# Float32 weights in two VectorE operations on 512-column tiles, and the first block's queries loaded four tokens to a row

## The chip, the cores and the metric

The kernel runs on one core of a Trainium2 chip. The metric is device time in microseconds, the median of several executions of one program; less is better. The profile comes from one execution.

## The reference

Attention over pooled keys and values, then two feed-forward layers, all in float32 on 4608 tokens of 512 features:

```python
# q, k, v: batch 8, heads 8, seq 576, head_dim 64; keys and values are pooled by 8, so 72 of each
k_p = k.reshape(B, H, Sp, 8, D).mean(axis=3)
v_p = v.reshape(B, H, Sp, 8, D).mean(axis=3)
scores = scale * np.matmul(q, k_p.transpose(0, 1, 3, 2))
attn = softmax(scores)                      # less the maximum, 1e-9 added to the sum
x = (attn @ v_p) -> (4608, 512)
h = x @ w_in                                # 512 x 2048
x = (h * np.clip(h + 3.0, 0.0, 6.0) / 6.0) @ w_out
g = x @ w_gate                              # 512 x 1536
out = (g * sigmoid(g) * (x @ w_val)) @ w_out2
```

The weights arrive as float64: each is two 32-bit words, and the kernel makes float32 of them on the chip.

## The kernel before

The tokens are cut into nine blocks of 512. **Startup** computes attention for block 0, in units of two heads (a pair, four pairs in all) and 256 tokens. In **block j** the first feed-forward layer runs over 16 slices f of 128 hidden columns: `up` (12 matmuls of 512 columns, line 553) makes a slice, `act1` and `split_g` its activation and its high and low part, and `down1` (12 matmuls) adds the slice of two steps earlier to four PSUM accumulators. Between them `attn_slot` puts the attention steps of block j + 1. Block 8 has no attention beside it. After block 8 (1040.6 us) the second layer runs on seven products in place of eight (lines 660 to 783).

A float32 matmul is made of three `float32r` matmuls on high and low parts (`mm3`), so every weight is split: ScalarE casts it to the high part, another engine subtracts (line 137).

Weights of the first layer come in during startup and block 0, by the class `Weights`. Its `todo` lists pieces of 256 columns (`WC`), two to each slice of `w_in` and two to each of `w_out`. They go through four stages: `fetch` starts a DMA into a tile of the pool `stg` (six tiles); `rescale` (line 115) has ScalarE multiply the upper words, read as float32, by 2^-112 in place; `join` (lines 117 to 133) has VectorE put the upper and lower words together with three integer operations; `split` casts on ScalarE and subtracts on GpSimd. Each call of `convert(2)` moves two pieces by one stage: it splits those joined in the call before, joins those rescaled, rescales two staged ones and refills the staging tiles. The joined pieces lie in the tiles `w32` of pool `t` (two buffers). Startup calls `convert` six times as step C of its plan, then until the second slice of `w_in` is there; block 0 calls it twice in each f. The high and low parts of `w_out` are also stored to DRAM (`w1d`) and read again in each later block.

Weights of the second layer are prepared in blocks 1 to 8 by `prep_slot`: 18 units, six f apart, of four quarters with 256 columns each; a unit is fetched, rescaled, joined (step 2), summed on GpSimd, cast on ScalarE and subtracted on VectorE, and stored.

All engines take their instructions in the order in which the program writes them. The order of attention steps comes from two tables (`when_startup`, `when`, lines 823 to 832): a unit i puts a step at slot i plus a lag, sorted by the second number within the slot. In startup a slot holds among others: X (exponentials of the unit before), T (transposes of the attention weights), K and P (transposes of a pair's pooled keys and of its queries), C (convert), V (attend), S (scores and their maximum).

The queries of the first block's four pairs are fetched by `load_first` (line 337): four DMAs a pair, each 512 tokens by 32 features, so rows of 128 bytes; the first two pairs' first two go out from ScalarE's queue, the others from SyncE's (SP). VectorE turns them with one transpose of 32 x 32 blocks (line 432) into `qT`, features by tokens. In startup the PSUM pool `ps_a` (two banks, tag `att`) serves only the transposes of the keys.

## Time and profile before

| | us |
|---|---|
| median of 3 runs | 1835.23 (1834.75 to 1835.96) |
| profiled execution | 1835.06 |
| its span, first to last instruction | 1833.3 |
| TensorE busy | 1748.5 (95%) |
| VectorE busy | 1258.8 (69%) |
| ScalarE busy | 686.8 (37%) |
| GpSimd busy | 676.6 (37%) |

The names in rows are those of the program: PE is TensorE, PEld its weight loads, DVE VectorE, ACT ScalarE, POOL GpSimd, SP SyncE; `L131` is line 131; `w<-wstg,w` writes tile `w` (for `w32`) and reads `wstg` and `w`. Idle time of an engine that is not the bottleneck costs nothing. An execution takes 1.8 us more than the span.

### The profile page before, as it was taken

How to read it: one execution, taken by the hardware profiler on the slowest of the kernel's cores; microseconds unless marked ns; L12 is line 12 of the kernel's file. 1: busy time of each engine (PE TensorE's matmuls, PEld its weight loads, DVE VectorE, ACT ScalarE, POOL GpSimd, SP SyncE). 2: the span in 40 equal slices, each digit the busy share in tenths (PEclk: the TensorE clock that was granted, in tenths of full speed). 3: DMA queues.
4: the chain of work that ended last, by engine and by line, in shares of the span. 5: the costliest groups of instructions: out<-in, count | busy, mean ns of one | idle time of the engine just before them, and what ended most of it. 6: DMA issues, size and time to landing. Idle time of an engine off the chain costs nothing.

```text
span 1833.3 us, 28479 instructions
## 1 busy us (share of the span) xinstructions
PE 1748.5 (95%) x9929; PEld 1575.9 (86%) x9929; DVE 1258.8 (69%) x2480; ACT 686.8 (37%) x1612; POOL 676.6 (37%) x833
## 2 busy tenths in 40 slices
PE   4687899999999998999999999999999999999999
PEld 3476688888878787878888899999999999999999
DVE  6787676876767677686542367767678668568666
ACT  5444344443444444444433223224224225124223
POOL 5455342331423325233114154153252352361450
PEclk8888999999999999999999999999999999999999
DMA  7555456665766656656553487887887977977876
GB/s 159 173 174 162 148 172 200 216 185 183 215 206 197 197 168 195 209 159 197 194 177 132 177 294 238 296 288 241 305 277 252 315 262 250 324 252 253 284 245 219
DMA packets 203103, 402.97 MB, mean 220 GB/s; under 512 B 90576, under 2 KB 126416, under 8 KB 192208
## 3 DMA queue, kind: packets, MB, share of 16 engines
q1 hardware_dynamic: 198256, 396.17, 66.9%
q10 hardware_dynamic: 4704, 4.98, 0.9%
q8 instruction: 79, 1.29, 0.3%
q14 instruction: 64, 0.52, 0.1%
HBM read 340.79 MB, written 60.29 MB: 219 GB/s over the span
## 4 chain that ended last, share of the span: by engine, by line
PE 81%; DVE 7%; DMA 5%; issue 2%; POOL 2%; ACT 2%; SPq 1%; ACTq 0%; POOLq 0%; DVEq 0%
PE b L660 43%; PE y L553 17%; PE h L553 16%; PE pss L445 2%; DMA y<-yo 1%; DVE w L126 1%; DVE w L131 1%; DMA vts<-in_v_dram 1%; PE pst L505 1%; DMA qs<-in_q_dram 1%; DVE w L120 1%; PE pst L509 1%; DVE kp L370 1%; DMA fly<-w1d 1%; PE psk L393 1%
## 5 line engine op out<-in xcount | busy, mean ns | idle before, releaser
L660 PE MATMUL b<-xc,wr 128*128 128x384 f32 x3024 | 525.2, 334 | 0.0
L660 PEld LDWEIGHTS b<-xc,wr 128*128 128x128 f32 x3024 | 524.0, 188 | 0.1
L553 PE MATMUL h<-x,wu 128*128 128x512 f32 x1728 | 435.3, 401 | 0.0
L553 PE MATMUL y<-g,fly 128*128 128x512 f32 x1728 | 430.2, 398 | 1.5 <-DMA fly<-w1d 0.8
L669 DVE TENSOR_TENSOR c<-c,b 128x384 f32<-128x384 f32 x504 | 265.2, 552 | 178.5 <-PE b L660 154.7
L553 PEld LDWEIGHTS h<-x,wu 128*128 128x128 f32 x1728 | 322.0, 191 | 65.3 <-DVE x L546 0.6
L553 PEld LDWEIGHTS y<-g,fly 128*128 128x128 f32 x1728 | 318.3, 189 | 66.4 <-ACT yo L594 1.0
L707 POOL TENSOR_TENSOR s<-s,c 128x384 f32<-128x384 f32 x144 | 142.4, 1013 | 400.2 <-ACT s L705 400.2
L660 PE MATMUL b<-wr,gc 128*128 128x256 f32 x2268 | 265.6, 279 | 0.0
L660 PEld LDWEIGHTS b<-wr,gc 128*128 128x128 f32 x2268 | 265.4, 188 | 0.0
L488 POOL TENSOR_TENSOR e<-e,sm 96x288 f32<-96x288 f32 (+3 forms) x85 | 73.5, 865 | 451.9 <-DVE sm L484 336.1
L714 POOL TENSOR_TENSOR gf<-s,c 128x384 f32<-128x384 f32 x144 | 168.2, 1192 | 67.3 <-DVE c L669 66.5
L136 ACT CAST gc<-gf 128x768 fp32r<-128x768 f32 x126 | 105.7, 839 | 186.6 <-POOL gf L714 101.0
L705 ACT ACTIVATE s<-c 128x384 f32<-128x384 f32 x144 | 73.5, 526 | 202.0 <-DVE c L669 200.9
L137 DVE TENSOR_TENSOR gc<-gf,gc 128x768 fp32r<-128x768 f32 x126 | 133.9, 1095 | 15.5 <-ACT gc L136 13.7
L137 DVE TENSOR_TENSOR g<-g,g 128x512 fp32r<-128x512 f32 x128 | 93.0, 727 | 67.1 <-ACT g L136 66.6
L577 DVE SCALAR_TENSOR_TENSOR g<-t,h 128x512 f32<-128x512 f32 x144 | 97.3, 676 | 59.9 <-ACT t L575 53.5
L136 ACT CAST g<-g 128x512 fp32r<-128x512 f32 x144 | 88.6, 615 | 85.5 <-PE y L553 46.0
L575 ACT ACTIVATE t<-h,three 128x512 f32<-128x512 f32 x144 | 98.2, 682 | 37.1 <-PE h L553 36.4
L475 ACT ACTIVATE e<-e 96x288 f32<-96x288 f32 (+3 forms) x85 | 35.3, 415 | 185.2 <-DVE e L472 183.9
L445 PE MATMUL pss<-kbd,qT 128*128 128x144 f32 (+2 forms) x336 | 63.2, 308 | 29.3 <-DVE x L546 26.4
L677 ACT COPY c<-b 128x384 f32<-128x384 f32 x72 | 33.9, 471 | 145.6 <-PE b L660 145.6
(106 smaller groups left out, 1723.0 us busy)
## 6 DMA issues: line engine op xcount, KB each, us to landing
wr<-sup SPq DMA_DIRECT2D x72, 1024.0 KB
fly<-w1d SPq DMA_DIRECT2D x128, 512.0 KB
wr<-sdn SPq DMA_DIRECT2D x84, 768.0 KB
wr<-sup SPq DMA_DIRECT2D x72, 768.0 KB
sup<-s SPq DMA_DIRECT2D x12, 1792.0 KB
wstg<-in_moe_w_out_dram SPq DMA_DIRECT2D x56, 256.0 KB
sdn<-s SPq DMA_DIRECT2D x6, 1792.0 KB
ystg<-y SPq DMA_DIRECT2D x24, 384.0 KB
```

Of the source, the lines that this page charges most:

```text
L136: nc.scalar.copy(out=hi, in_=src)
L137: lo_engine.tensor_tensor(out=lo, in0=src, in1=f32(hi), op=ALU.subtract)
L445: nc.tensor.matmul(out=ps[:, i], lhsT=qT[:, i * qt:(i + 1) * qt], rhs=kbd_t[p], start=True, stop=True)
L488: nc.gpsimd.tensor_tensor(out=e3, in0=e3, in1=sm.to_broadcast(list(e3.shape)), op=ALU.mult)
L553: nc.tensor.matmul(out=ps, lhsT=w(kt, wh), rhs=x(kt, xh), start=first and n == 0, stop=last and n == 3 * len(kts) - 1,)
L575: nc.scalar.activation(out=t, in_=ps, func=ACTF.Relu, bias=three)
L577: nc.vector.scalar_tensor_tensor(out=g, in0=t, scalar=6.0, in1=ps, op0=ALU.min, op1=ALU.mult)
L660: nc.tensor.matmul(out=ps, lhsT=w(wh), rhs=x(xh), start=first and n == 0, stop=last and n == 2)
L669: add = lambda dst, a, b: nc.vector.tensor_tensor(out=dst, in0=a, in1=b, op=ALU.add)
L705: nc.scalar.activation(out=g[q], in_=c[q], func=ACTF.Sigmoid)
L707: nc.gpsimd.tensor_tensor(out=g[q], in0=g[q], in1=c[q], op=ALU.mult)
L714: nc.gpsimd.tensor_tensor(out=gf[p][:, GP[TURN[q]], f], in0=g[q], in1=c[q], op=ALU.mult)
```

## The change

- A piece is 512 columns, a whole slice: `WC` is 512, `stg` has three tiles, `convert(1)` moves one piece by one stage. Each of `w_in`'s and `w_out`'s 32 slices is one DMA.
- `rescale` uses the function `Prelu` in place of `Copy`: positive values are multiplied by 2^-112, negative ones by 2^-112 times 2^32. `join` then needs one shift by 3 to the left and one operation that shifts the lower word and combines it; the third operation, which put the sign back, is gone.
- The units of the second layer take two staging tiles of two quarters each, by the same four DMAs, and join two quarters at once into two places of `q7`.
- The queries of the first block's four pairs come in one DMA a pair, four tokens (1 KB) of one head to a partition. `prep_q` turns them for these pairs with eight TensorE matmuls against the identity into one PSUM bank, and VectorE copies the bank to `qT` with the tokens back in order.

```diff
@@ -77,7 +77,7 @@
...
     prep_ctx = ExitStack()
-    stg_p = prep_ctx.enter_context(tc.tile_pool(name="stg", bufs=6, side="right"))
+    stg_p = prep_ctx.enter_context(tc.tile_pool(name="stg", bufs=3, side="right"))
     q7_p = prep_ctx.enter_context(tc.tile_pool(name="q7", bufs=1, side="right"))
@@ -97,40 +97,38 @@
     wu = {}
-    WC = 256
+    WC = 512
     def fetch(src):
         t = stg_p.tile([P, WC, 2], F32, tag="stg", name="wstg")
+        fetch_into(t, src)
+        return t
+    def fetch_into(t, src):
         nc.sync.dma_start(
...
         )
-        return t
     def rescale(stage):
         hi = stage[:, :, 1]
-        nc.scalar.activation(out=hi, in_=hi, func=ACTF.Copy, scale=2.0 ** -112)
-    def join(pieces):
-        for stage, dst in pieces:
-            hi = stage[:, :, 1].bitcast(I32)
-            nc.vector.tensor_scalar(
-                out=dst, in0=hi, scalar1=4, scalar2=1,
-                op0=ALU.logical_shift_left, op1=ALU.logical_shift_right,
-            )
-        for stage, dst in pieces:
-            lo = stage[:, :, 0].bitcast(I32)
-            nc.vector.scalar_tensor_tensor(
-                out=dst, in0=lo, scalar=29, in1=dst, op0=ALU.logical_shift_right, op1=ALU.bitwise_or
-            )
-        for stage, dst in pieces:
-            hi = stage[:, :, 1].bitcast(I32)
-            nc.vector.scalar_tensor_tensor(
-                out=dst, in0=hi, scalar=-(2 ** 31), in1=dst, op0=ALU.bitwise_and, op1=ALU.bitwise_or
-            )
+        nc.scalar.activation(out=hi, in_=hi, func=ACTF.Prelu, scale=2.0 ** -112, alpha=2.0 ** 32)
+    def join(stage, dst, parts=1):
+        hi, lo = (stage[:, :, i].bitcast(I32) for i in (1, 0))
+        if parts > 1:
+            hi, lo = (t.rearrange("p (k n) -> p k n", k=parts) for t in (hi, lo))
+        nc.vector.tensor_scalar(
+            out=dst, in0=hi, scalar1=3, scalar2=None, op0=ALU.logical_shift_left,
+        )
+        nc.vector.scalar_tensor_tensor(
+            out=dst, in0=lo, scalar=29, in1=dst, op0=ALU.logical_shift_right, op1=ALU.bitwise_or
+        )
     def split(hi, lo, src, lo_engine):
@@ -141,50 +139,36 @@
...
             self.todo, self.staged, self.scaled, self.joined = [], [], [], []
-            self.cur = {}
         def add_up(self, key, src, f):
             w = src.bitcast(I32).rearrange("(k p) f -> p k f", p=P)[:, :, 2 * P * f:2 * P * (f + 1)]
-            for i in range(KT * P // WC):
-                m = WC // P
-                self.todo.append(("up", key, w[:, m * i:m * (i + 1)], i))
+            self.todo.append(("up", key, w))
         def add_down(self, key, src, f):
-            w = src.bitcast(I32)[f * P:(f + 1) * P, :]
-            for i in range(DM // WC):
-                self.todo.append(("down", key, w[:, 2 * WC * i:2 * WC * (i + 1)], i))
+            self.todo.append(("down", key, src.bitcast(I32)[f * P:(f + 1) * P, :]))
         def fetch(self):
-            while self.todo and len(self.staged) + len(self.scaled) < 6:
+            while self.todo and len(self.staged) + len(self.scaled) < 3:
                 item = self.todo.pop(0)
...
             done, self.joined = self.joined, []
-            for (kind, key, _, i), t in done:
-                if i == 0:
-                    if kind == "up":
-                        self.cur[key] = wu_p.tile([P, 2, KT, P], F32R, tag="wu", name="wu")
-                    else:
-                        self.cur[key] = fly_p.tile([P, 2, DM], F32R, tag="fly", name="fly")
-                w = self.cur[key]
+            for (kind, key, _), t in done:
                 if kind == "up":
+                    w = wu[key] = wu_p.tile([P, 2, KT, P], F32R, tag="wu", name="wu")
                     w = w.rearrange("p a k f -> p a (k f)")
-                w = w[:, :, WC * i:WC * (i + 1)]
+                else:
+                    w = fly[key] = fly_p.tile([P, 2, DM], F32R, tag="fly", name="fly")
                 split(w[:, 0], w[:, 1], f32(t), nc.gpsimd)
-                if i == KT * P // WC - 1:
-                    t = self.cur.pop(key)
-                    (wu if kind == "up" else fly)[key] = t
-                    if kind == "down":
-                        nc.sync.dma_start(out=w1_d[key[1]], in_=f32(t))
-            pieces = []
+                if kind == "down":
+                    nc.sync.dma_start(out=w1_d[key[1]], in_=f32(w))
             scaled, self.scaled = self.scaled, []
...
                 t = t_p.tile([P, WC], I32, tag="w32", name="w32")
-                pieces.append((s, t))
+                join(s, t)
                 self.joined.append((item, t))
-            join(pieces)
             for item, s in self.staged[:n]:
@@ -222,6 +206,7 @@
...
     PREP = 6
+    WH = WC // 2
     prep_t = {}
@@ -236,21 +221,26 @@
...
             prep_t["q", u] = []
-            for quarter in ("11", "12", "21", "22"):
-                r, c = int(quarter[0]) - 1, int(quarter[1]) - 1
-                if kind == "up":
-                    w = (w_gate, w_val)[m].bitcast(I32).rearrange("(k p) f -> p k f", p=P)
-                    src = w[:, 2 * c:2 * c + 2, 2 * P * (2 * f + r):2 * P * (2 * f + r + 1)]
-                else:
-                    w = w_out2.bitcast(I32)[P * (2 * f + r):P * (2 * f + r + 1), :]
-                    src = w[:, 4 * P * c:4 * P * (c + 1)]
-                prep_t["q", u].append((fetch(src), place[quarter]))
+            for pair in ((("11", "21"), ("12", "22")) if kind == "up" else (("11", "21"), ("22", "12"))):
+                t = stg_p.tile([P, WC, 2], F32, tag="stg", name="wstg")
+                for i, quarter in enumerate(pair):
+                    r, c = int(quarter[0]) - 1, int(quarter[1]) - 1
+                    if kind == "up":
+                        w = (w_gate, w_val)[m].bitcast(I32).rearrange("(k p) f -> p k f", p=P)
+                        src = w[:, 2 * c:2 * c + 2, 2 * P * (2 * f + r):2 * P * (2 * f + r + 1)]
+                    else:
+                        w = w_out2.bitcast(I32)[P * (2 * f + r):P * (2 * f + r + 1), :]
+                        src = w[:, 4 * P * c:4 * P * (c + 1)]
+                    fetch_into(t[:, WH * i:WH * (i + 1)], src)
+                a, b = (place[quarter] for quarter in pair)
+                prep_t["q", u].append((t, slice(a, b + 1, b - a)))
         elif step == 1:
...
         elif step == 2:
-            q = prep_t["f", u] = q7_p.tile([P, 8, WC], F32, tag="q7", name="q7")
-            join([(s, q[:, i].bitcast(I32)) for s, i in prep_t.pop(("q", u))])
+            q = prep_t["f", u] = q7_p.tile([P, 8, WH], F32, tag="q7", name="q7")
+            for s, at in prep_t.pop(("q", u)):
+                join(s, q[:, at].bitcast(I32), 2)
         elif step == 3:
@@ -258,7 +248,7 @@
...
         elif step == 4:
-            q, t = prep_t["f", u], s7_p.tile([P, 7, 2, WC], F32R, tag="s7", name="s7")
+            q, t = prep_t["f", u], s7_p.tile([P, 7, 2, WH], F32R, tag="s7", name="s7")
             prep_t["s", u] = t
@@ -284,6 +274,7 @@
...
     MAXQ = 2
+    QJ = N // P
     kbd_t = [a_p.tile([P, K2], F32, name=f"kbd{p}") for p in range(KT)]
@@ -333,8 +324,11 @@
...
             k_t[0, p] = [ks[p][:SP_, h2] for h2 in range(2)]
-            t = qs[p // 2][:, p % 2].rearrange("p o (c d) -> p (o c) d", d=32)
-            fetch_q(t, (0, p, 0, seg_n), [nc.scalar, nc.scalar, nc.sync, nc.sync] if p < 2 else sync4)
+            t = qs[p // 2][:, p % 2].rearrange("p (h j) d -> p h j d", h=2)
+            (nc.scalar if p == 0 else nc.sync).dma_start(
+                out=t.rearrange("p h j d -> p h (j d)"),
+                in_=q[0, 2 * p:2 * p + 2, :seg_n].rearrange("h (p j) d -> p h (j d)", p=P),
+            )
             q_t[0, p, 0, seg_n] = t
@@ -429,6 +423,17 @@
...
         t = a_p.tile([P, N // 32, 32], F32, tag="qT", name="qT", bufs=2)
+        if seg in segs[:KT]:
+            s, ps = q_t.pop(seg), psum("k", [P, QJ, P])
+            for j in range(QJ):
+                for h2 in range(2):
+                    nc.tensor.matmul(
+                        out=ps[D * h2:D * (h2 + 1), j], lhsT=s[:, h2, j], rhs=ident, start=True, stop=True
+                    )
+            qT_t[seg] = t.rearrange("p c s -> p (c s)")
+            nc.vector.tensor_copy(out=qT_t[seg].rearrange("d (p j) -> d j p", j=QJ), in_=ps)
+            return
         nc.vector.transpose(out=t[:, :n // 32], in_=q_t.pop(seg)[:, :n // 32])
@@ -946,7 +951,7 @@
...
         elif what == "C":
-            weights.convert(2)
+            weights.convert()
         elif what == "E":
@@ -993,7 +998,7 @@
...
         while ("in", 1) not in wu:
-            weights.convert(2)
+            weights.convert()
         def attn_slot(j, s):
@@ -1033,7 +1038,7 @@
...
             g = act1(hp)
-            weights.convert(2 if j == 0 else 0)
+            weights.convert(1 if j == 0 else 0)
             if n >= 2:
@@ -1041,7 +1046,7 @@
...
             split_g((1, j, f), g)
-            weights.convert(2 if j == 0 else 0)
+            weights.convert(1 if j == 0 else 0)
             if j > 0:
```

## Rows read from the trace of the kernel before

**Rows 1.** The page, second part: TensorE's busy share in the span's 40 equal slices (45.8 us each), in tenths, 9 for 90% and more.

```profile
...
PE   4687899999999998999999999999999999999999
...
```

**Rows 2.** Busy time of each engine by stretch: the stretch and its length, then busy us and number of instructions of TensorE's matmuls, its weight loads, VectorE, ScalarE and GpSimd, then the granted TensorE clock, the DMA queues' busy share and GB/s. The stretches are startup, block 0, blocks 1, 2 and 5 and, last, blocks 1 to 6 together.

```profile
...
0.00:56.40 56.40, 26.24 (x112) 18.97 (x113) 38.05 (x117) 30.07 (x139) 29.29 (x63) 0.80 0.78 167
56.40:212.20 155.80, 120.53 (x578) 96.68 (x578) 121.21 (x287) 71.63 (x214) 86.44 (x119) 0.90 0.51 161
212.20:317.20 105.00, 104.19 (x521) 86.13 (x520) 74.65 (x173) 44.44 (x120) 34.63 (x55) 1.00 0.58 181
317.20:421.60 104.40, 103.28 (x517) 85.98 (x516) 78.09 (x186) 47.55 (x125) 34.84 (x58) 1.00 0.64 194
630.40:741.80 111.40, 104.82 (x517) 85.87 (x516) 78.83 (x186) 47.00 (x125) 40.13 (x58) 1.00 0.60 184
...
212.20:849.90 637.70, 622.27 (x3069) 512.90 (x3068) 462.00 (x1060) 272.76 (x719) 212.85 (x332) 1.00 0.63 193
...
```

**Rows 3.** Groups of VectorE's instructions in block 0: line, engine, operation, tiles, shapes and count, then busy us, mean ns of one, and idle us in front of them with what ended it.

```profile
...
L120 DVE TENSOR_SCALAR w<-wstg 128x256 int32<-128x256 int32 x56 | 31.4, 600 | 26.6 <-POOL wu L137 18.2 <-POOL fly L137 5.4 <-DMA q_in<-in_q_dram 2.8
L131 DVE SCALAR_TENSOR_TENSOR w<-wstg,w 128x256 int32<-128x256 int32 x56 | 27.6, 531 | 0.0
L126 DVE SCALAR_TENSOR_TENSOR w<-wstg,w 128x256 int32<-128x256 int32 x56 | 25.7, 497 | 0.0
...
```

**Rows 4.** Who waited for whom in block 0: us in all, times, longest us.

```profile
...
PE pss L445 <- DVE x L546: 20.6, 6, 4.7
...
DVE w L120 <- POOL wu L137: 18.2, 11, 2.8
...
DVE w L120 <- POOL fly L137: 5.4, 8, 1.0
...
```

**Rows 5.** Single lines over the whole span: engine, operation, tiles and count, then min/median/max ns of one, first and last start in us, shapes.

```profile
L120 DVE TENSOR_SCALAR w<-wstg x64: 279/797/1371, 34.3 to 203.2; 128x256 int32<-128x256 int32 x64
...
L131 DVE SCALAR_TENSOR_TENSOR w<-wstg,w x64: 408/412/1779, 35.7 to 205.5; 128x256 int32<-128x256 int32 x64
...
L577 DVE SCALAR_TENSOR_TENSOR g<-t,h x144: 651/678/691, 64.4 to 1033.2; 128x512 f32<-128x512 f32 x144
...
L137 POOL TENSOR_TENSOR wu<-w,wu x32: 716/728/926, 38.9 to 199.0; 128x256 fp32r<-128x256 f32 x32
...
L137 POOL TENSOR_TENSOR g<-g,g x16: 1252/1295/1584, 66.9 to 213.1; 128x512 fp32r<-128x512 f32 x16
```

**Rows 6.** Groups of GpSimd's instructions in block 0, columns as in rows 3.

```profile
...
L137 POOL TENSOR_TENSOR fly<-w,fly 128x256 fp32r<-128x256 f32 x30 | 21.6, 741 | 15.9 <-ACT fly L136 15.9
L137 POOL TENSOR_TENSOR wu<-w,wu 128x256 fp32r<-128x256 f32 x28 | 20.3, 747 | 4.2 <-ACT wu L136 4.2
...
```

**Rows 7.** The chain of waits in order of time, from 0 to 260 us: start us, us, what, here two pieces of TensorE.

```profile
...
92.90 3.65 PE psk L393 x32
...
239.26 2.75 PE h L553 x12
...
```

**Rows 8.** Groups of the whole span with different shapes kept apart, columns as in rows 3.

```profile
...
L115 ACT ACTIVATE wstg<-wstg 128x256 f32<-128x256 f32 x136 | 49.7, 430 | 0.0
...
L126 DVE SCALAR_TENSOR_TENSOR q<-wstg,q 128x256 int32<-128x256 int32 x72 | 28.4, 453 | 0.0
...
L131 DVE SCALAR_TENSOR_TENSOR q<-wstg,q 128x256 int32<-128x256 int32 x72 | 26.1, 421 | 0.0
...
L120 DVE TENSOR_SCALAR q<-wstg 128x256 int32<-128x256 int32 x72 | 21.4, 357 | 0.0
...
L592 DVE TENSOR_SCALAR yo<-y 128x512 f32<-128x512 f32 x18 | 12.1, 684 | 5.0 <-PE y L553 4.9
...
L968 ACT ACT_TABLE_LOAD x1 | 1.3, 1283 | 0.8 <-PEq L1107 0.8
...
L1051 ACT ACT_TABLE_LOAD x1 | 1.3, 1283 | 0.0
...
```

**Rows 9.** The chain of waits by line, as shares of a stretch: first from 0 to 34.2 us, then from 34 to 56.4 us (SPq and ACTq are the engines' own DMA queues, issue is time in which the profile shows no wait).

```profile
by line: DMA qs<-in_q_dram 32.5%; DMA wstg<-in_moe_w_out_dram 15.7%; DMA vt<-in_v_dram 12.7%; SPq L311 11.7%; DMA q_in<-in_q_dram 9.2%; SPq L104 7.3%; SPq L312 2.2%; issue 2.1%; ACT L968 1.7%; ACTq L361 1.5%; SPq L361 0.9%; DVE qT L432 0.7%
...
by line: DVE w L120 13.2%; DVE w L126 12.7%; DVE w L131 11.1%; issue 9.0%; POOL wu L137 6.5%; DVE x L546 6.0%; ACT es L468 5.9%; DVE mx L451 5.1%; ACT wu L136 4.0%; DVE aT L525 4.0%; POOL fly L137 3.1%; DVE es L472 2.9%; PE psv L532 2.6%; P
...
```

**Rows 10.** Busy time by stretch in startup, columns as in rows 2.

```profile
...
0.00:10.00 10.00, 2.39 (x9) 2.13 (x9) 4.27 (x13) 2.11 (x5) 3.92 (x14) 1.00 0.88 119
...
20.00:30.00 10.00, 6.08 (x37) 4.30 (x36) 8.36 (x23) 7.88 (x41) 7.44 (x16) 1.00 1.01 251
...
```

**Rows 11.** The DMA queues from 0 to 10 us: packets, bytes and how many packets are small.

```profile
...
DMA packets 3643, 1.19 MB, mean 119 GB/s; under 512 B 3253, under 2 KB 3253, under 8 KB 3643
...
```

**Rows 12.** Groups of the first 36 us with shapes kept apart, columns as in rows 3.

```profile
...
L445 PE MATMUL pss<-kbd,qT 128*128 128x144 f32 x32 | 7.6, 383 | 2.9 <-ACT kbd L399 2.9
...
L432 DVE STREAM_TRANSPOSE qT<-qs 128x512 f32<-128x512 f32 x4 | 2.8, 702 | 0.0
...
```

**Rows 13.** What TensorE waited for from 212 to 1040 us: us in all, times, longest us.

```profile
...
PE pss L445 <- DVE x L546: 5.7, 6, 2.1
PE psv L534 <- DVE vtl L424: 4.3, 3, 2.5
...
```

## Prediction

> **What bounds the kernel now.** Three views are enough, in this order. The page's forty slices [rows 1] show TensorE at 4 to 8 tenths in the first five slices and at 9 after that, so nearly all that can be gained lies in the first 230 us. The stretches [rows 2], cut at the first `up` matmul of each block, put numbers on it: startup lasts 56.4 us, block 0 lasts 155.8 us with 35.3 us of TensorE idle and a granted clock of 0.90, while block 1 lasts 105.0 us at clock 1.00 and is TensorE's own. The six blocks that convert second-layer weights (212.2 to 849.9 us) hold 15.4 us of TensorE idle together.
>
> The third view says what holds block 0. VectorE is busy for 121.2 us [rows 2]; the three lines of `join` are 31.4 + 25.7 + 27.6 = 84.7 us of that, and VectorE waits 26.6 us more in front of line 120, the first of them [rows 3]. 121.2 + 26.6 is 148 of 155.8 us: VectorE is the bound there. The wait is mostly for GpSimd's low-part subtraction of the piece joined before (18.2 + 5.4 us) [rows 4]: a `convert` makes two pieces and there are two `w32` buffers, so each join writes over a piece that GpSimd still reads. TensorE then waits behind the joins: 20.6 us for VectorE's line 546, which stands after them in the queue [rows 4].
>
> **The change, part by part.**
>
> *Joins of block 0.* 56 records of each line are 28 converts. One costs VectorE 84.7 / 28 = 3.02 us now, plus 26.6 / 28 = 0.95 us of waiting. After, it is one shift and one or-combination on 512 columns. The combination is the operation of line 577 at its width: 0.68 us (bounds: 0.65, that line's minimum; 0.82, twice the 0.41 of 256 columns) [rows 5]. The shift on 512 columns has no row: 0.28 us if width cost nothing, 0.56 us for two of 256; I take the middle, 0.42. That is 1.10 us undisturbed, 28 x 1.10 = 31 us. With one piece per convert and two buffers, a join only needs the subtraction of the piece before the last, a whole convert earlier, so I let the 23.6 us of waiting for GpSimd go.
>
> Undisturbed is too good: line 120 takes 0.28 us at best and 0.80 us at the median, and one GpSimd subtraction (0.73 us) lies between [rows 5]. Some of that collision is built in today, since the join starts when the first of two subtractions ends and the second begins. After, GpSimd has 86.4 - 41.9 + 28 x 1.30 = 81 us of work in block 0 (its 512-column subtraction takes 1.30 us) [rows 2, 5, 6]. At some 70% load and 1 us an operation, an operation of VectorE that arrives anywhere loses about 0.35 to 0.45 us: 56 of them, 20 to 25 us. VectorE then needs 121.2 - 84.7 + 31 + 0 to 25 = 67 to 92 us.
>
> The Trainium skill has a rule that speaks against the change (SBUF — State Buffer, "Who interferes with whom"): GpSimd and a VectorE operation in a two-port mode or with two SBUF inputs lock each other out for a whole instruction. By it GpSimd's operations of double width block for longer, and at its worst that is rival B, 1813 us. The trace agrees that such a lock exists (line 120 at 0.28 and at 0.80 us), and its medians for the combinations, at their undisturbed 0.41, say that it is rarely met there.
>
> TensorE's floor in block 0: 192 `up` and 168 `down` matmuls at 2.75 us per 12 are 82.5 us; the 96 records that pool three heads' keys, at 3.65 us per 32, are 10.9 us; the attention of block 1's kind is 104.2 - 384 / 12 x 2.75 = 16.2 us [rows 2, 7]. Sum 109.6 us. The worst later block (630.4 to 741.8 us) idles 6.6 us with VectorE at 71% [rows 2]; I give block 0 the same: 116 us, so **39.6 us less**. If TensorE still waited for line 546 as long as today (20.6 us), 130 us; if nothing stalls it, 109.6.
>
> What covers the rest of block 0: ScalarE is busy 71.6 of 155.8 us, and one `Prelu` on 512 columns for two copies of 0.43 us [rows 8] lies between 0.43 (width free) and twice 0.86; 28 x 0.86 = 24 us at worst would still fit beside TensorE. Casts and subtractions of 512 cost a little less than two of 256 and are counted above. Staging keeps its bytes (three tiles of 512 for six of 256) and its look-ahead of two converts; SP issues half the weight DMAs, but a tile is asked for and released as one.
>
> *Joins of startup.* Four converts join between 34.0 and 56.4 us. The three lines hold 13.2 + 12.7 + 11.1 = 37.0% of the chain in these 22.4 us, 8.3 us, and GpSimd's subtractions another 9.6%, 2.2 us [rows 9]. Four joins at 1.10 us, without GpSimd and some issue time around it, make it **7 us less** (bounds 0, if units hang on something else, and 10).
>
> *Queries of the first block.* 16 DMAs of 64 KB in 128-byte rows become four of 256 KB in 1 KB rows; SP issues three instead of twelve. In 0 to 10 us the queues are 88% busy and move 119 GB/s, in 20 to 30 us they are full at 251 GB/s [rows 10]. At the second rate (4.0 us per MB) the 0.77 MB of larger packets of the first stretch take 3.1 us, so its 3253 small ones [rows 11] took 5.7 us. 8192 of them are 14 us; as large packets the 1.05 MB are 4.2 us: up to 10 us of DMA time saved. The chain to 34 us is nearly all DMA and SP [rows 9]. But TensorE gets eight fp32 matmuls per pair, 64 records in all (16 matmuls of line 393 show 32 records): 7.3 us at 114 ns each [rows 7], 15 us at the 237 ns of line 445 in startup [rows 12]. Behind them in TensorE's queue stand the pair's key transpose, the attend of an earlier unit and the scores, and ScalarE's exponentials wait for those. The VectorE copy out of PSUM (512 columns, like line 592's 0.68 us) replaces a transpose of 0.70 us [rows 8, 12], so nothing is saved there. The PSUM bank comes from the two that only key transposes use in startup, and is asked for once per pair, so I give it nothing. Bounds -10 and +15. VectorE is busy 8.4 and ScalarE 7.9 of 10 us between 20 and 30 us [rows 10], so an earlier arrival meets engines with little slack, while TensorE is idle more than half of startup. I let them cancel: **0**.
>
> *Second-layer weights.* A unit's twelve joins (357, 453 and 421 ns mean [rows 8]) are 4.9 us; four of 512 are 2.2 us. 18 units free 49 us of VectorE, but of TensorE's 15.4 us of idle in those blocks and the few after, 5.7 is line 546 behind VectorE's queue and 4.3 line 424's tail of V, which ScalarE and GpSimd set from a DMA [rows 13]. I take half the first: **3 us less** (bounds 8 less, 2 more). From 1040.6 us on nothing is touched.
>
> **Sum.** 39.6 + 7 + 0 + 3 = 49.6 us. The profiled execution took 1835.06 us (span 1833.3 and 1.8 around it), 0.17 below the median: 1835.1 - 49.6 = 1785.5, forecast **1785 us**.
>
> **Rivals.**
>
> B, GpSimd's longer operations hold VectorE. If each of 56 operations waits for a whole 1.30 us subtraction, joins cost 28 x (1.10 + 2.6) = 104 us, VectorE 140 us, block 0 about 144: 12 + 7 + 3 = 22 us saved, **1813 us**. For it: line 131's 1.78 us maximum [rows 5]. Against: its median is the free 0.41.
>
> C, weights come late. Block 0 moves 155.8 us x 161 GB/s = 25.1 MB; at the 194 GB/s of block 2 [rows 2], 129 us: 27 + 7 + 3 = 37 us, **1798 us**. For it: weight transfers hold part of startup's chain [rows 9]. Against: the queues are 51% busy [rows 2], 79 us, which is 69% of 116.
>
> D, slower: `Prelu` may need another activation table than `Exp`. The only two table loads are 1.28 us each [rows 8], one for `Exp` and one for the later `Sigmoid`. Were it so, ScalarE would load twice wherever converts and exponentials alternate: 4 times in startup, 12 in block 0, 18 in the units after, 34 x 2.57 = 87 us. All of it on the path gives 1785 + 87 = **1872 us**; it turns the sign when more than 19 of the 34 are not hidden. Against: `Copy` and `Relu` run between exponentials without a load.
> On this the Trainium skill (ScalarE: Activation LUTs, "Table sets: the hidden batching unit") says that cheap functions such as relu sit in every set; it doesn't list this one by name, and no run here has it.
>
> E, the joins turn out not to be on the path and the rest cancels: 1835 us. F, the whole 10 us of DMA time counts, block 0 reaches its floor of 109.6, and 3 us more go in the later blocks: 1785 - 10 - 6 - 3 = 1766 us.
>
> **How the numbers follow.** Forecast 0.62 (1771 to 1800), B 0.15, C 0.13, D 0.04, E 0.02, F 0.04. The range 1767 to 1812 leaves out F's far half, B's upper half, D, E and little of the forecast's edges: under 0.2. 0.2% is 3.7 us, about what a measurement here can tell from no change. Faster is all but D and E: 0.94; same 0.02; slower 0.04.
>
> **What would show it.** Right: block 0 at 110 to 125 us with clock near 1.00; no wait of the join for GpSimd; shift and combination near 0.42 and 0.68 us at their minimum; the first `up` matmul at 45 to 54 us; no table load beyond two; blocks 1 to 8 shorter by a few us. Wrong: joins with medians above 1.3 us (B), a rescale that waits for its transfer and TensorE for weights (C), loads beside line 115 (D), a first `up` matmul after 56 us (the turn on TensorE costs more than the packets gave).

## The result and the profile after

| | before | after |
|---|---|---|
| median, measured side by side (4 runs each) | 1835.60 (1834.75 to 1837.52) | 1786.32 (1781.32 to 1787.76) |
| ratio to before, 95% interval | | 0.9725 (0.9705 to 0.9746) |
| profiled execution / its span | 1835.06 / 1833.3 | 1787.76 / 1786.0 |
| startup (to the first `up` matmul) | 56.4 | 52.2 |
| block 0 | 155.8 | 120.7 |
| blocks 1 to 8 and the tail of the first layer | 828.2 | 820.0 |
| second layer | 792.9 | 793.1 |

All in us. The changed kernel is faster by 49 us; 1785 was forecast. The stages are cut as in the prediction, at the first `up` matmul of each block, and they show that the total hides errors of both signs: startup gave 4.2 us, block 0 gave 35.1 and the rest of the first layer 8.2.

First the page of the kernel after, second part: TensorE's busy tenths in 40 slices of 44.7 us.

```profile
PE   6899999999999999999999999999999999999999
```

The weak slices at the head are two where there were five [rows 1]. Next the stretches of after, with the columns of [rows 2]: startup, block 0, and blocks 1 to 6 together.

```profile
0.00:52.20 52.20, 32.43 (x177) 24.46 (x178) 38.41 (x101) 29.78 (x130) 29.66 (x60) 0.90 0.70 178
52.20:172.90 120.70, 113.04 (x578) 92.40 (x578) 104.76 (x175) 66.68 (x159) 88.56 (x90) 0.93 0.68 209
...
172.90:802.40 629.50, 622.78 (x3069) 515.25 (x3068) 439.93 (x934) 271.30 (x687) 210.33 (x333) 0.99 0.63 195
```

TensorE's idle time in block 0 fell from 35.3 to 7.7 us, in blocks 1 to 6 from 15.4 to 6.7. VectorE is still busy for 104.8 of 120.7 us in block 0. Its work there shrank by 16 us, while 54 of the join's 84.7 us [rows 3] were to go. The groups of VectorE in block 0 say why (columns of [rows 3]):

```profile
L129 DVE SCALAR_TENSOR_TENSOR w<-wstg,w 128x512 int32<-128x512 int32 x28 | 42.0, 1502 | 1.0
L126 DVE TENSOR_SCALAR w<-wstg 128x512 int32<-128x512 int32 x28 | 19.5, 696 | 3.7 <-POOL wu L135 3.6
```

and the single lines over the whole span for the first layer's weights (columns of [rows 5]; line 126 is the shift, line 129 the combination):

```profile
L126 DVE TENSOR_SCALAR w<-wstg x32: 398/426/2105, 34.8 to 164.5; 128x512 int32<-128x512 int32 x32
...
L129 DVE SCALAR_TENSOR_TENSOR w<-wstg,w x32: 691/1110/3522, 35.5 to 164.9; 128x512 int32<-128x512 int32 x32
```

The wait in front of the join is 3.7 us, where it was 26.6. The undisturbed times are 0.40 and 0.69 us, as estimated (0.42 and 0.68). But in block 0 the two lines together take 61.5 us, twice the 31 us of undisturbed work. The timeline (start us, us, engine, line, operation, tiles) shows one of the worst combinations with what GpSimd ran under it:

```profile
151.69 1.35 POOL L401 TENSOR_TENSOR vts<-vts 96x128 f32<-96x128 f32 x2
...
152.45 0.41 DVE L126 TENSOR_SCALAR w<-wstg 128x512 int32<-128x512 int32 x1
...
152.90 3.21 DVE L129 SCALAR_TENSOR_TENSOR w<-wstg,w 128x512 int32<-128x512 int32 x1
153.01 1.29 POOL L135 TENSOR_TENSOR g<-g,g 128x512 fp32r<-128x512 f32 x1
154.27 1.29 POOL L135 TENSOR_TENSOR wu<-w,wu 128x512 fp32r<-128x512 f32 x1
```

The shift is free and takes 0.41 us. The combination that follows starts at 152.90 us, while GpSimd is at the end of line 401 (to 153.04), and ends at 156.11. Two GpSimd subtractions begin and end under it, one behind the other without a gap, the second at 155.56: 0.55 us are left after that, and the whole takes 3.21 us for 0.69 us of work. Here a GpSimd operation's end did not let VectorE in, since the next one stood ready.

Who waited in block 0 (columns of [rows 4]):

```profile
ACT wstg L120 <- DMA wstg<-in_moe_w_out_dram: 4.1, 4, 1.9
...
DVE w L126 <- POOL wu L135: 3.6, 4, 1.4
...
PE pss L450 <- DVE x L551: 1.2, 2, 0.6
```

TensorE's 20.6 us behind the attention output (`x`, now line 551) are 1.2 us. The rescale waits for its DMA for 4.1 us, and TensorE waits for no weight.

### The profile page after: what moved, and what is told of

Same layout as the page of the kernel before. It is cut to its first block, busy times and chain, and to the rows that moved or that the text cites. A ratio compares the mean times of both kernels' runs of the same rounds, so it can differ in the third digit from the quotient of the medians.

```text
span 1786.0 us, 28146 instructions
## 1 busy us (share of the span) xinstructions
PE 1747.7 (98%) x9993; PEld 1579.5 (88%) x9993; DVE 1216.1 (68%) x2208; ACT 679.4 (38%) x1512; POOL 674.8 (38%) x801
## 3 DMA queue, kind: packets, MB, share of 16 engines
q8 instruction: 79, 1.29, 0.3%
## 4 chain that ended last, share of the span: by engine, by line
PE 91%; DVE 3%; DMA 2%; issue 2%; ACT 1%; POOL 1%; SPq 0%; ACTq 0%; DVEq 0%; POOLq 0%
PE b L665 44%; PE y L558 21%; PE h L558 20%; PE pss L450 2%; DMA y<-yo 1%; PE pst L514 1%; PE pst L510 1%; PE psv L539 1%; PE psv L537 1%; PE psv L538 1%; DVE w L126 1%; PE psk L387 0%; PE psv L536 0%; DMA qs<-in_q_dram 0%; DMA vts<-in_v_dram 0%
## 5 line engine op out<-in xcount | busy, mean ns | idle before, releaser
L134 ACT CAST g<-g 128x512 fp32r<-128x512 f32 x144 | 88.6, 615 | 69.5 <-PE y L558 50.1
L480 ACT ACTIVATE e<-e 96x288 f32<-96x288 f32 (+3 forms) x85 | 35.3, 415 | 164.9 <-DVE e L477 162.9
L199 DVE TENSOR_TENSOR gf<-gf 128x768 f32<-128x768 f32 (+1 forms) x66 | 66.9, 1029 | 12.1 <-POOL gf L719 10.9
```

What stands on the lines that cost most here:

```text
L134: nc.scalar.copy(out=hi, in_=src)
L199: eng.tensor_tensor(out=v(what), in0=v(a), in1=v(b), op=op)
```

## The experiments

Each kernel's time is a median over three rounds; its ratio is against the kernel before, run beside it on the same chip (medians 1835.6 to 1837.4), with a 95% interval. "The changed kernel" stands at 0.9725 (0.9705 to 0.9746). Stage lengths are startup / block 0 / rest of the first layer, each from one profile; startup of three kernels with the same code there (the changed kernel, `g_vector`, `prep_three`) differed between 49.9 and 52.3 us, so startup differences below about 2 us are not read.

### The two halves of the change apart

`q_alone`: the kernel before with only the changed query loading and its turn on TensorE.

```diff
-            t = qs[p // 2][:, p % 2].rearrange("p o (c d) -> p (o c) d", d=32)
-            fetch_q(t, (0, p, 0, seg_n), [nc.scalar, nc.scalar, nc.sync, nc.sync] if p < 2 else sync4)
+            t = qs[p // 2][:, p % 2].rearrange("p (h j) d -> p h j d", h=2)
+            (nc.scalar if p == 0 else nc.sync).dma_start(
+                out=t.rearrange("p h j d -> p h (j d)"),
...
+        if seg in segs[:KT]:
...
```

> The kernel before with only the new loading and turning of the first block's queries. If DMA time saved and TensorE time added cancel, as forecast: first `up` at 55 to 58 us, total 1835 +- 4 us. Rival: the startup's gain of 4 us seen in the changed kernel is the queries' alone: first `up` at 52 us, total 1829 to 1832 us.

Measured: 1838.01 us, 1.0002 (0.9992 to 1.0011); 57.5 / 157.0 / 829.2.

`w_alone`: the changed kernel with the query part undone, the same diff the other way round.

> The changed kernel with the old loading and turning of the queries. Forecast: the weights carry everything, 1786 +- 4 us. Rival, the queries carry part of startup: 1790 to 1795 us, first `up` at 55 us or later.

Measured: 1788.79 us, 0.9733 (0.9716 to 0.9749); 52.1 / 121.1 / 820.6.

The weights carry all of the gain, and the queries are worth nothing within the interval. That zero has two parts. `q_no_turn` keeps the larger rows but turns them with the old transpose on VectorE; it leaves out putting the tokens of block 0 back in order, so only its time is read.

```diff
         if seg in segs[:KT]:
-            s, ps = q_t.pop(seg), psum("k", [P, QJ, P])
-            for j in range(QJ):
-                for h2 in range(2):
-                    nc.tensor.matmul(
-                        out=ps[D * h2:D * (h2 + 1), j], lhsT=s[:, h2, j], rhs=ident, start=True, stop=True
-                    )
+            s = q_t.pop(seg).rearrange("p h j (c d) -> p (h j c) d", d=32)
+            nc.vector.transpose(out=t, in_=s)
             qT_t[seg] = t.rearrange("p c s -> p (c s)")
-            nc.vector.tensor_copy(out=qT_t[seg].rearrange("d (p j) -> d j p", j=QJ), in_=ps)
             return
```

> The changed kernel with the new loading of the first block's queries but the old VectorE transpose in place of TensorE's turn; the queries of block 0 then stand at other places, so that part of the output differs. If the larger packets gain time and the turn takes it back, the first `up` comes 2 to 6 us earlier than in the changed kernel: 46 to 50 us in place of 52, total 1780 to 1784 us. Rival, neither counts, because startup hangs on its engines: 51 to 53 us, total 1784 to 1788 us.

Measured: 1784.79 us, 0.9710 (0.9692 to 0.9729); 48.6 / 120.9 / 823.0. Startup is 3.5 us shorter than in `w_alone` (52.1), the gain of the larger rows, and 3.6 us shorter than in the changed kernel (52.2), the price of the turn. Each figure compares one profile with one profile, so by the spread above it is good to some 2 us. The total doesn't show either: it missed its forecast of 1780 to 1784 us, its later blocks were 3 us longer in this profile, and its interval overlaps those of `w_alone` and of the changed kernel. The DMA queues carry the rows faster. Kernel after, its first 10 us, columns as in [rows 10]:

```profile
0.00:10.00 10.00, 2.47 (x18) 1.99 (x19) 4.27 (x12) 1.93 (x4) 5.42 (x17) 1.00 0.73 163
```

They are 73% busy and move 163 GB/s, where they were 88% busy for 119 [rows 10]. The other side are the groups of the kernel after in startup, columns as in [rows 3]: the scores, the turn's matmuls (line 431) and VectorE's copy of their result out of PSUM.

```profile
L450 PE MATMUL pss<-kbd,qT 128*128 128x144 f32 x32 | 8.0, 400 | 2.8 <-DVE qT L435 1.5 <-ACT kbd L393 1.3
L431 PE MATMUL psk<-ident,qs 128*64 128x128 f32 x64 | 7.0, 390 | 6.6 <-DMA qs<-in_q_dram 6.6
...
L435 DVE COPY qT<-psk 128x512 f32<-128x512 f32 x4 | 4.3, 1064 | 4.6 <-PE psk L431 4.6
```

The matmuls take 7.0 us (7.3 at the low end of the estimate) and the copy 1.06 us, where a transpose took 0.70 [rows 12] and 0.68 was assumed from line 592. The copy's output goes to every fourth token; whether that is what makes it slower was not tried. Would more matmuls cost more? `q_turn_twice` computes the turn twice.

```diff
+            for _ in range(2):
                 for j in range(QJ):
                     for h2 in range(2):
...
```

> The changed kernel with each of the 32 matmuls that turn the first block's queries done twice, 64 more records, 7 us of TensorE in startup. If the turn is on the path, the first `up` comes 4 to 7 us later, 56 to 59 us, total 1790 to 1794 us. Rival, it hides: 52 to 54 us, total 1785 to 1788 us.

Measured: 1789.44 us, 0.9743 (0.9724 to 0.9761), 52.1 us of startup: no longer than with one, and a total between the two forecasts. The same groups of this kernel:

```profile
L432 PE MATMUL psk<-ident,qs 128*64 128x128 f32 x128 | 9.2, 306 | 5.9 <-DMA qs<-in_q_dram 5.9
...
L451 PE MATMUL pss<-kbd,qT 128*128 128x144 f32 x32 | 5.4, 296 | 3.9 <-ACT kbd L393 1.8 <-DVE qT L436 1.6 <-ACT x L548 0.5
```

Twice the records take 9.2 us, not 14.0, and the scores behind them 5.4 us, not 8.0. So this kernel doesn't price a matmul of the turn; what it found is told in the last section.

### What holds the join: the buffer, the third operation, the lock

`w32_four`: the kernel before with four tiles `w32`, so that a join needn't wait for GpSimd to finish with the piece before.

```diff
-                t = t_p.tile([P, WC], I32, tag="w32", name="w32")
+                t = t_p.tile([P, WC], I32, tag="w32", name="w32", bufs=4)
```

> The kernel before with four w32 buffers in place of two and nothing else, so that no join waits for GpSimd's subtraction of the call before; the three operations on 256 columns stay. If the 24 us of waiting are lost time, block 0 falls by 15 to 24 us: 1811 to 1820 us. If the wait only moves (the joins then collide with GpSimd instead), 1828 to 1836 us.

Measured: 1828.60 us, 0.9953 (0.9938 to 0.9968); 55.0 / 149.8 / 831.2. Its groups of VectorE in block 0:

```profile
L126 DVE SCALAR_TENSOR_TENSOR w<-wstg,w 128x256 int32<-128x256 int32 x56 | 41.6, 782 | 0.0
L131 DVE SCALAR_TENSOR_TENSOR w<-wstg,w 128x256 int32<-128x256 int32 x56 | 33.4, 635 | 0.0
L120 DVE TENSOR_SCALAR w<-wstg 128x256 int32<-128x256 int32 x56 | 30.1, 577 | 0.1
```

The wait of 26.6 us [rows 3] is gone, 0.1 is left, but the two combinations went from 53.3 to 75.0 us. Most of the wait came back as longer operations, and block 0 gained only 6 us: a join that starts earlier starts while GpSimd is at work.

`w32_one`: the changed kernel with a single tile `w32`, which brings the wait back.

```diff
-                t = t_p.tile([P, WC], I32, tag="w32", name="w32")
+                t = t_p.tile([P, WC], I32, tag="w32", name="w32", bufs=1)
```

> The changed kernel with one w32 buffer in place of two, so that each join again waits for GpSimd's subtraction of the piece before. The wait comes back with at least the 24 us of the kernel before; four buffers there gave 9 us, so if it is a like loss here: block 0 at 126 to 138 us, total 1792 to 1806 us. Rival, the wait only takes the place of the collisions: 120 to 125 us, total 1785 to 1790 us.

Measured: 1813.87 us, 0.9875 (0.9860 to 0.9889); 52.9 / 145.3 / 819.4. Its groups of VectorE in block 0:

```profile
L129 DVE SCALAR_TENSOR_TENSOR w<-wstg,w 128x512 int32<-128x512 int32 x28 | 22.8, 813 | 1.0
L126 DVE TENSOR_SCALAR w<-wstg 128x512 int32<-128x512 int32 x28 | 16.7, 597 | 48.6 <-POOL wu L135 27.9 <-POOL fly L135 18.2 <-DMA vts<-in_v_dram 2.5
```

The mirror of the run before: 48.6 us of waiting, and the combinations, which now start when GpSimd has just ended, take 0.81 us in place of 1.50. The pair of tiles is worth 24.6 us of block 0 in the changed kernel. The loss is larger than either forecast allowed (126 to 138 us, and 120 to 125). So the wait must go for the change to pay, and letting it go by itself doesn't pay much.

`three_ops`: the changed kernel with 512 columns and two buffers, but with `Copy` and the three old operations in every join.

```diff
-        nc.scalar.activation(out=hi, in_=hi, func=ACTF.Prelu, scale=2.0 ** -112, alpha=2.0 ** 32)
+        nc.scalar.activation(out=hi, in_=hi, func=ACTF.Copy, scale=2.0 ** -112)
...
-            out=dst, in0=hi, scalar1=3, scalar2=None, op0=ALU.logical_shift_left,
+            out=dst, in0=hi, scalar1=4, scalar2=1,
+            op0=ALU.logical_shift_left, op1=ALU.logical_shift_right,
...
+        nc.vector.scalar_tensor_tensor(
+            out=dst, in0=hi, scalar=-(2 ** 31), in1=dst, op0=ALU.bitwise_and, op1=ALU.bitwise_or
+        )
```

> The changed kernel with the old arithmetic on 512 columns: Copy in rescale and three operations in join, everything else as changed. One more combination of 0.7 to 1.5 us in each of 28 joins of block 0 is 19 to 42 us of VectorE, which was busy 105 of 121 us there: block 0 at 135 to 150 us, total 1802 to 1818 us. Rival, the gain is the wait and the wider tiles alone and the third operation hides: 1786 to 1792 us.

Measured: 1817.79 us, 0.9897 (0.9883 to 0.9912); 54.4 / 142.0 / 825.7. Its joins in block 0:

```profile
L130 DVE SCALAR_TENSOR_TENSOR w<-wstg,w 128x512 int32<-128x512 int32 x28 | 35.9, 1282 | 1.0
L133 DVE SCALAR_TENSOR_TENSOR w<-wstg,w 128x512 int32<-128x512 int32 x28 | 30.4, 1086 | 1.0
L126 DVE TENSOR_SCALAR w<-wstg 128x512 int32<-128x512 int32 x28 | 21.5, 769 | 0.7 <-POOL wu L139 0.7
```

Without the two-operation join the rest of the change takes 19 us off the kernel before (1836.6 - 1817.8). The buffers alone gave 8 (`w32_four`); the width of 512 by itself was not tried. The third operation is the other 31 (1817.8 - 1786.3), 21.3 of them in block 0 and 5.7 behind it. Its own row is 30.4 us in block 0, where 28 x 0.69 = 19 would be undisturbed; the three rows together are 87.8 us where the two were 61.5. The rescale takes as long with `Copy` as with `Prelu` (675 and 672 ns at the median), so it is not what differs.

`lo_vector`: the changed kernel with the first layer's weight subtraction on VectorE, which takes GpSimd's work in block 0 from 88.6 to 51.8 us.

```diff
-                split(w[:, 0], w[:, 1], f32(t), nc.gpsimd)
+                split(w[:, 0], w[:, 1], f32(t), nc.vector)
```

> The changed kernel with the weights' low parts of startup and block 0 subtracted on VectorE in place of GpSimd. If the joins lose their time to GpSimd's operations (30 us of the 61 in block 0), the combination's mean falls from 1.50 to 0.8 to 1.0 us, which pays for the 28 subtractions of 0.69 us (19 us) that VectorE takes over: VectorE busy 98 to 105 us, block 0 116 to 122 us, total 1780 to 1789 us. Rival, the combination is slow for another reason (strided words, its width): mean stays above 1.4 us, block 0 over 132 us, total 1798 us or more.

Measured: 1789.44 us, 0.9748 (0.9733 to 0.9762); 51.2 / 123.0 / 820.0. Its block 0, first the stretch, then, in a second view, the groups of VectorE:

```profile
51.20:174.20 123.00, 112.37 (x579) 91.09 (x578) 106.61 (x204) 66.75 (x159) 51.78 (x61) 0.94 0.70 211
```

```profile
L129 DVE SCALAR_TENSOR_TENSOR w<-wstg,w 128x512 int32<-128x512 int32 x28 | 23.1, 826 | 1.0
L126 DVE TENSOR_SCALAR w<-wstg 128x512 int32<-128x512 int32 x28 | 19.8, 705 | 0.0
L135 DVE TENSOR_TENSOR wu<-w,wu 128x512 fp32r<-128x512 f32 x14 | 12.1, 862 | 2.8 <-ACT wu L134 2.8
L135 DVE TENSOR_TENSOR fly<-w,fly 128x512 fp32r<-128x512 f32 x15 | 11.4, 762 | 2.5 <-ACT fly L134 2.5
```

With GpSimd busy for 51.8 us in place of 88.6, the combination takes 0.83 us in place of 1.50, with the same strided words and the same width. So it is GpSimd's work that stretches it, and the rival is out. But the subtractions cost VectorE 23.5 us, a little more than the 18.9 us that came back, and block 0 is 2.3 us longer: VectorE's time (106.6 us), block 0 and the total all came out just above their forecasts. The shift stays at 0.70 us on average, so its losses don't come from these subtractions alone.

`g_vector`: the other tenant of GpSimd goes instead, the activation's low part in block 0.

```diff
-        split(gt[:, 0], gt[:, 1], g, nc.gpsimd if key[:2] == (1, 0) else nc.vector)
+        split(gt[:, 0], gt[:, 1], g, nc.vector)
```

> The changed kernel with the activation's low part of block 0 subtracted on VectorE (as in the later blocks) in place of GpSimd. GpSimd loses 22 of 89 us in block 0, VectorE takes 16 x 0.69 = 11 us. By the lock the joins lose a quarter less (some 8 us): VectorE busy 103 to 109 us, block 0 117 to 123 us, total 1782 to 1790 us. Rival, no such lock: VectorE 116 us, block 0 128 us, total 1794 us.

Measured: 1783.22 us, 0.9709 (0.9695 to 0.9724); 49.9 / 117.6 / 817.5. The combination takes 1.26 us. Block 0 gains 3 us, but the intervals of this kernel and the changed one overlap.

`lo_halves`: GpSimd's weight subtraction as two operations of 256 columns, so that VectorE could come in between.

```diff
-                split(w[:, 0], w[:, 1], f32(t), nc.gpsimd)
+                nc.scalar.copy(out=w[:, 0], in_=f32(t))
+                for at in (slice(0, WC // 2), slice(WC // 2, WC)):
+                    nc.gpsimd.tensor_tensor(
+                        out=w[:, 1, at], in0=f32(t)[:, at], in1=f32(w[:, 0, at]), op=ALU.subtract
+                    )
```

> The changed kernel with GpSimd's subtraction of a weight piece in two operations of 256 columns. If VectorE waits for the one GpSimd operation that is running when it comes, shorter ones halve that part of the loss: combination's mean 1.1 to 1.3 us, block 0 115 to 119 us, total 1779 to 1785 us. Rival, GpSimd's next operation takes the lock again, so its total time counts and not the length of one: mean 1.4 to 1.6 us, block 0 120 to 125 us, total 1785 to 1792 us.

Measured: 1784.95 us, 0.9725 (0.9710 to 0.9739); 50.5 / 120.1 / 819.7. The combination takes 1.29 us, but the shift 0.79 in place of 0.70 and the join waits 5.7 us in place of 3.7. That lies between its two forecasts, and it is no gain by itself.

`g_vec_halves` has both edits.

> The changed kernel with both edits that shortened block 0 by a little: the activation's low part of block 0 on VectorE, and GpSimd's subtraction of a weight piece in two operations of 256 columns. If they add: startup 50 us, block 0 115 to 118 us, total 1779 to 1783 us. Rival, block 0 is at TensorE's floor and what is left of the lock: no better than the first edit alone, 1782 to 1785 us.

Measured: 1779.06 us, 0.9685 (0.9669 to 0.9701); 52.3 / 114.9 / 818.8. It is the fastest kernel here, 7 us under the changed one, and its interval lies below the changed kernel's. Its block 0:

```profile
52.30:167.20 114.90, 109.47 (x579) 89.53 (x579) 102.23 (x190) 66.32 (x159) 78.64 (x104) 0.96 0.72 220
```

and two of its groups of VectorE there, which answer to the 42.0 and 19.5 us of after:

```profile
L129 DVE SCALAR_TENSOR_TENSOR w<-wstg,w 128x512 int32<-128x512 int32 x28 | 31.0, 1108 | 1.0
L126 DVE TENSOR_SCALAR w<-wstg 128x512 int32<-128x512 int32 x28 | 20.5, 731 | 0.1
```

TensorE's work is 109.5 us, with 5.4 us of idle. In the changed kernel it was 113.0 and 7.7. That 109.5 is so near the floor of the prediction (109.6) is luck, as told below.

### The second layer's weights

`prep_three`: the changed kernel, with `Copy` and three operations for the second layer's weights alone (the diff of `three_ops`, in the units of `prep_slot`; `rescale(s, True)` is the `Copy` of before).

```diff
-                rescale(s)
+                rescale(s, True)
...
             hi, lo = (t.rearrange("p (k n) -> p k n", k=parts) for t in (hi, lo))
+            nc.vector.tensor_scalar(
+                out=dst, in0=hi, scalar1=4, scalar2=1,
+                op0=ALU.logical_shift_left, op1=ALU.logical_shift_right,
+            )
...
+            return
```

> The changed kernel with Copy and the three-operation join for the second layer's weights alone (36 more operations of 0.69 us, 25 us of VectorE over blocks 1 to 7). If the 8 us that the later blocks lost come from VectorE's shorter queue there, startup and block 0 stay at 173 us and the rest of the first layer is 823 to 827 us in place of 820, total 1788 to 1794 us. Rival, they come from elsewhere: 820 us and 1786 us.

Measured: 1793.76 us, 0.9776 (0.9760 to 0.9793); 52.3 / 120.5 / 825.8. Startup and block 0 are as in the changed kernel, and the blocks after are 5.8 us longer. Its blocks 1 to 6, and in a second view what TensorE waits for from block 1 to the end of the first layer:

```profile
172.80:808.10 635.30, 622.27 (x3070) 512.89 (x3069) 460.93 (x964) 270.43 (x687) 212.46 (x331) 1.00 0.64 193
```

```profile
PE pss L464 <- DVE x L565: 5.0, 5, 2.4
PE psv L553 <- DVE vtl L432: 3.3, 3, 1.4
```

And the same view of the changed kernel:

```profile
PE pss L450 <- DVE x L551: 2.4, 1, 2.4
...
PE psv L539 <- DVE vtl L418: 1.6, 1, 1.6
```

TensorE idles 13.0 us in these six blocks with three operations and 6.7 with two; its busy time is the same to 0.5 us. The second layer's joins hold VectorE for 73.5 us here and for 47.3 in the changed kernel (sums of their groups); of the 26 us between them 6 reach TensorE, 4.3 of these through the two waits shown.

## Why the forecast came out right, and where its steps did not

**What bounds the kernel: right.** VectorE held block 0, and TensorE is now busy for 113.0 of 120.7 us there. The wait behind line 546 went from 20.6 to 1.2 us with the joins.

**Joins of block 0: 39.6 us forecast, 35.1 measured.** The undisturbed prices were right to 0.02 us. Two things were not.
- The loss to GpSimd was put at 0 to 25 us, from 0.35 to 0.45 us an operation. It was 61.5 - 31 = 30 us, 0.55 us an operation, and VectorE was busy for 104.8 us, not 67 to 92. The estimate let an operation lose one collision; the timeline shows operations that lose to two GpSimd operations in a row. Four of the 28 combinations took over 3 us, and these four lost 10.6 of the 30 us. The Trainium skill's rule says how long one operation blocks (SBUF — State Buffer, "Who interferes with whom": the engine that issues first has the shared ports for the whole instruction and the other blocks). That GpSimd gets them again ahead of a waiting VectorE is what the row at 152.90 us shows, with 3.21 us for 0.69 us of work. A second error stands in the same sum: the three old rows of the join, 84.7 us, overlap in time. VectorE was at work on `wstg` in block 0 for 80.4 us in all, so the rest of its work was 41 us and not the 36.5 that the subtraction gave; after, it is 104.8 - 61.5 = 43.3.
- TensorE's floor of 109.6 us mixes two clocks. The 3.65 us for 32 records that pool keys [rows 7] come from a stretch at the lower level, while the 2.75 us per 12 are from one at full clock. In the kernel before the same 32 records also ran at full clock, as these stretches (columns of [rows 2]) show:

```profile
92.90:96.55 3.65, 3.65 (x33) 3.50 (x33) 2.20 (x6) 2.31 (x7) 2.22 (x4) 0.50 0.43 137
121.67:123.69 2.02, 2.02 (x34) 1.94 (x33) 0.00 (x0) 0.75 (x3) 2.02 (x3) 1.00 0.05 20
```

At 2.02 us the three heads are 6.1 us and the floor at full clock is 104.8. What TensorE took beyond it is the clock: less the share of the stretch that was not granted, the work of block 0 is 120.5 - 0.10 x 155.8 = 104.9 us in the kernel before, 113.0 - 0.07 x 120.7 = 104.6 after and 109.5 - 0.04 x 114.9 = 104.9 in `g_vec_halves`. So the forecast's 109.6 has some 5 us of low clock in it by accident, where the kernel after had 8.

By the sum, 3.4 of the 4.5 us that block 0 missed by (120.7 for 116.2) are TensorE's work and 1.1 are idle (7.7 for 6.6). But one profile speaks against the clock as the cause. `prep_three` runs the same code in block 0, and there the clock was higher and the block no shorter:

```profile
52.30:172.80 120.50, 110.23 (x579) 89.48 (x578) 107.27 (x175) 66.83 (x159) 87.77 (x90) 0.96 0.68 211
```

TensorE's 2.8 us less of work came back as idle time (10.3 us). The block got shorter where GpSimd had less to do and VectorE's queue with it (114.9 us in `g_vec_halves`, VectorE at 102.2), which points to the first error as the step that cost the 4.5 us. One low stretch of the kernel after, from 70 us on, stands behind a pause:

```profile
70.00:82.00 12.00, 9.33 (x64) 7.67 (x62) 9.24 (x18) 7.47 (x17) 11.26 (x13) 0.91 0.85 239
82.00:92.00 10.00, 10.00 (x39) 8.20 (x39) 9.80 (x15) 5.27 (x14) 6.69 (x7) 0.77 0.57 197
92.00:105.00 13.00, 13.00 (x89) 11.14 (x88) 11.15 (x18) 8.42 (x20) 11.34 (x14) 1.00 0.72 224
```

TensorE idles 2.7 us in the first stretch; in the second it is busy without a break, part of it at the lower level of 1.2 GHz (0.77 on average), and in the third it has the full 2.4 GHz again.

**The 23.6 us of wait that were let go: right only as part of the whole.** Alone, the buffers gave 8.0 us (`w32_four`, 1836.6 - 1828.6); one taken away from the changed kernel cost 27.6 (`w32_one`). A wait for an engine and a collision with it are partly the same time, and the step counted the wait as free and the collision as a surcharge. It came out because the change also took away two of three operations that can collide (56 in place of 168).

**Joins of startup: 7 us forecast, 4.2 measured.** On the chain between 34.9 and 36.6 us the shift takes 0.58 us and the combination 1.10, not 0.42 and 0.68. The chain by line from 34 to 52.2 us (as in [rows 9]) says what else is there:

```profile
by line: DMA v_in<-in_v_dram 17.9%; issue 11.6%; DVE w L129 10.3%; ACT es L473 7.2%; SPq L308 7.0%; DVE w L126 5.6%; DVE aT L530 5.0%; DVE mx L456 4.6%; SPq L302 4.1%; DVE x L551 4.1%; PE psv L537 4.1%; ACT wstg L120 3.8%; PE psv L538 2.4%;
...
```

The two join lines are 15.9% of 18.2 us, 2.9 us, where the three had 8.3, and GpSimd's subtractions are off the list; but a transfer of raw values now holds 17.9%, 3.3 us, and it is not among the entries shown of before [rows 9]. Whether the missing 2.8 us are this transfer or startup's own spread of some 2 us can't be told from these runs.

**Queries: 0 forecast, 0 measured, for the stated reason** as far as one profile of each kernel can tell. The gain of the rows (3.5 us, of up to 10) and the price of the turn (3.6 us) cancel. The lower price in the estimate, 114 ns a record, is one of the lower clock too; three of the four turns ran there (last section), so their 7.0 us come near its 7.3.

**Second-layer weights: 3 us forecast, 8.2 measured**, just past the bound of 8. The forecast halved the wait for line 546 and let nothing else go; `prep_three` shows that the tail of V waits for VectorE too (3.3 us with three operations, 1.6 with two). The step put that wait down to ScalarE and GpSimd. 5.8 of the 8.2 us are the third operation; what the wider operations and the staging add wasn't tried apart.

The terms that missed are 4.5 and 2.8 us too much and 5.2 too little: the profiled execution ended 2.3 us above its forecast (1787.76 for 1785.5) and the median 1.3 above, because these offset each other. That nearness is luck; the range was not.

**The rivals.** B (GpSimd's longer operations hold VectorE, 1813 us) had the right mechanism and too large a price: it charged 1.30 us to every operation, and 0.55 was lost. C (weights late, 1798 us) didn't come: the rescale waits 4.1 us for DMAs, and TensorE for no weight, though block 0 now draws 209 GB/s. D (table loads, 1872 us) didn't come either. These are the rows of the rescale and of the only two loads in the kernel after:

```profile
L120 ACT ACTIVATE wstg<-wstg x68: 647/672/696, 31.6 to 865.9; 128x512 f32<-128x512 f32 x68
```

```profile
L973 ACT ACT_TABLE_LOAD x1 | 1.3, 1283 | 0.8 <-PEq L1112 0.8
L1056 ACT ACT_TABLE_LOAD x1 | 1.3, 1283 | 0.0
```

`Prelu` on 512 columns takes 0.67 us, between the 0.43 and 0.86 that were given. The Trainium skill (ScalarE: Activation LUTs, "Table sets: the hidden batching unit") counts functions as cheap as relu to every set; these rows show that this one behaves like them beside `Exp`. E (1835 us) and F (1766 us) are out by the total.

## What to carry to other kernels

Before a wait for GpSimd is counted as gained, ask what VectorE will do in that time: if it starts a two-input integer operation while GpSimd has a queue of its own, the wait comes back as a longer operation, and what brought the time home here was fewer operations on either side. Price such an operation by its mean in a stretch where both engines are busy, not by its minimum or median. And where an edit is forecast at zero, say of which gain and which cost, and test each half by itself: here some 3.5 us of startup, by one profile each, are still to be had in the larger DMA rows by whoever finds a cheaper turn.

## What the runs showed that was not expected

The turn's matmuls ran at half the pace of the same matmuls done twice over. These two pieces of the timeline turn one pair's queries, the first in the kernel after, where two later rows are added, the second in `q_turn_twice`:

```profile
20.88 1.98 PE L431 MATMUL psk<-ident,qs 128*64 128x128 f32 x16
...
24.13 1.22 PE L450 MATMUL pss<-kbd,qT 128*128 128x144 f32 x4
...
27.16 0.66 PE L450 MATMUL pss<-kbd,qT 128*128 128x144 f32 x4
...
29.77 1.09 PE L431 MATMUL psk<-ident,qs 128*64 128x128 f32 x16
```

```profile
20.46 1.97 PE L432 MATMUL psk<-ident,qs 128*64 128x128 f32 x32
...
23.69 0.73 PE L451 MATMUL pss<-kbd,qT 128*128 128x144 f32 x4 [0.53 <-ACT x L548]
```

16 records in 1.98 us are 124 ns each, 32 in 1.97 us are 62 ns each, and the scores behind them took 1.22 and 0.73 us. It is the clock, although the granted-clock column reads 1.00 in both stretches. The column is made from the trace's clock records and counts the time before the first of them as 1.00. That first record, with 1.00, stands at 25.1 us in the kernel after and at 8.7 us in `q_turn_twice`. In the kernel after the pace changes there: the scores behind it take 0.66 us in place of 1.22, the last pair's turn 1.09 us in place of 1.98. This ratio, 1.8, is that of 3.65 to 2.02 us between granted clocks of 0.50 and 1.00. So TensorE ran at the lower level, 1.2 GHz, up to 25.1 us, three of the four turns with it, and the startup clocks of 0.90 above and 0.80 in [rows 2] are too high.

The first record is not at one place for one code: it stands at 25.1 us in the kernel after, at 18.2 in `g_vector` and at 14.0 in `prep_three`, whose startup is the same. So one profile doesn't show that the second set of matmuls brought it forward. What it does show is that a kernel with more matmuls need not have a longer startup, and that the price of a matmul can't be had by doubling it where the clock is not the same in both kernels.

The copy of 512 columns out of PSUM took 1.06 us with its output at every fourth element, where line 592's dense operation took 0.68 [rows 8]; the two were not compared in one kernel.
